# Moving one weight load between two DMA queues at the start of a linear-attention and GEGLU kernel, and reordering the first key matmuls to suit

## Chip, cores, metric

The kernel runs on one core of one Trainium2 chip. The metric is device time in microseconds (us), median of several executions. Before the change it was 273.76 us (three runs, 273.72 to 274.07). A profile's span is about 1.3 us shorter than the time of the same execution, because it counts from the first to the last instruction.

## The reference, cut to what matters

```python
x = A_x                                    # 1 x 2048 x 640, bf16
g = sigmoid((x * gate_w).sum(-1, keepdims=True))
# A: linear attention, 32 heads of 20; phi(t) = where(t > 0, t + 1, exp(t)) + 1e-6
q, k, v = split(x @ wqkv)                  # wqkv: 640 x 1920
a = (phi(q) @ (phi(k)^T v) / (phi(q) . sum phi(k))) @ wo
# B: gelu(x @ w_gate) * (x @ w_up) @ w_down, 640 -> 1728 -> 640
return g * a + (1 - g) * b
```

The change concerns only the first 8 us: the keys `x @ wk` of the first tiles of 128 tokens. wk is the 640 x 640 key part of wqkv; it is loaded in five chunks of 128 rows (160 KB each), one for each 128-deep step of the contraction. "x tile i" is 128 tokens.

## The kernel before: the parts that matter

The matmuls need x with its columns on the partitions. Tile 0 is loaded plainly and transposed by TensorE (`T`); all later tiles come by a transposing DMA (`load_xT`). Two engines issue the early loads, each in program order: SyncE ("sp", SPq in the profile) and ScalarE ("act", ACTq). Neither waits for anything there, so the order of these lines is the order of issue.

```python
def load_wk(k, eng="sp", after=()):
    dma_in(wk[:, k, :], A_wqkv[k * 128:(k + 1) * 128, 640:1280], [r_wk[k]], reads=after, eng=eng)   # issued at L341

def load_xT(i, after=()):
    P.op("sp", lambda e: e.dma_start_transpose(xT[:, :, i * 128:(i + 1) * 128],
                                               A_x[0, i * 128:(i + 1) * 128, :]), ...)              # L353
# ... (cut)
load_x(0)
load_wk(0)
load_xT(1)
load_wk(3)
load_wk(4)
load_wk(1, "act")
load_wk(2, "act")
# ... (cut: a dummy activation that loads ScalarE's table, the gate weights)
for i in range(2, NQ):          # NQ = 4: x tiles 2 and 3
    load_xT(i)
for k in range(KC):
    load_wq(k)
for i in range(NQ, NT):
    load_xT(i)
```

`KM(n, ks)` multiplies tile n by the chunks ks of wk: two matmuls for a chunk, 512 columns (L453) and 128 columns (L454), summed in PSUM (the buffer that takes the results of matmuls) over the five chunks. `warm` runs matmuls on constants, to have TensorE busy before data are there. The order on TensorE is:

```python
warm(5, 512)
warm(1, 128)
T(0, [0], 7)
T(0, [1, 2, 3, 4], 6)
warm(2, 128)
for k in range(3):
    KM(0, [k])
for k in range(3):
    KM(1, [k])
KM(0, [3])
KM(1, [3])
gate_col()
KM(0, [4])
KM(1, [4])
# then keys of tiles 2 and 3, queries of tiles 0 to 3, keys and queries of tiles 4 to 15, ...
```

Of the kernel before, what the change touches and what calls it, by code (L numbers as in the profile page):

```python
# [162 lines left out]
def bass_gated_mix__linear_attn_block__geglu_ffn__prompt_kernel(  # L163
# [63 lines left out]
    with (  # L227
# [8 lines left out]
        with contextlib.ExitStack() as stack:  # L236
# [12 lines left out]
            def new_dma_key():  # L249
                k = "in%d" % dma_next[0]  # L250
                dma_next[0] += 1
                return k
# [16 lines left out]
            wk = wkq[:, :, 0:640]  # L269
# [40 lines left out]
            r_wk = [P.sb("wk%d" % k, R_WK + k * WW, R_WK + k * WW + 640) for k in range(KC)]  # L310
# [29 lines left out]
            def dma_in(dst, src, writes, reads=(), eng="sp"):  # L340
                P.op(eng, lambda e, dst=dst, src=src: e.dma_start(dst, src),  # L341
                     reads=reads, writes=writes, dma=new_dma_key())
# [3 lines left out]
            def load_x(i, eng="sp"):  # L346
                dma_in(x_aug[:, i, 0:640], A_x[0, i * 128:(i + 1) * 128, :], [r_xn[i]], eng=eng)

            def load_wk(k, eng="sp", after=()):
                dma_in(wk[:, k, :], A_wqkv[k * 128:(k + 1) * 128, 640:1280], [r_wk[k]], reads=after, eng=eng)  # L350

            def load_xT(i, after=()):
                P.op("sp", lambda e: e.dma_start_transpose(xT[:, :, i * 128:(i + 1) * 128],  # L353
                                                           A_x[0, i * 128:(i + 1) * 128, :]),
                     reads=list(after), writes=[r_xT[i]], dma=new_dma_key())

            def load_wq(k, eng="sp"):
# [4 lines left out]
                 writes=[P.res("touch")], dma=new_dma_key())  # L362
            load_x(0)
            load_wk(0)
            load_xT(1)
            load_wk(3)
            load_wk(4)
            load_wk(1, "act")
            load_wk(2, "act")

            zero = nc.const_aps.tensor(0.0, (128, 1), F32)
            P.op("act", lambda e: e.activation(eg[:, 0:1], zero, ACT.Exp), writes=[r_eg[0]])
# [15 lines left out]
            for c in range(NHC):  # L388
# [9 lines left out]
                 reads=[r_ones], writes=[r_ident])  # L398
# [16 lines left out]
            def warm(count, n):  # L415
                def fn(e):
                    last = None
                    for w in range(count):
                        last = e.matmul(ps[:, 4, 0:n], one_l, one_r[:, 0:n], start=True, stop=True)
                    return last  # L420
                P.op("pe", fn, writes=[bank[4]])
# [4 lines left out]
            def slot(n):  # L426
                return SLOTS[n % 4]
# [17 lines left out]
            def KM(n, ks):  # L445
                i = seq[n][1]
                b0, b1 = slot(n)

                def fn(e):
                    last = None  # L450
                    for k in ks:
                        lhs = xT[:, k, i * 128:(i + 1) * 128]
                        e.matmul(ps[:, b0, :], lhs, wk[:, k, 0:512], start=(k == 0), stop=(k == KC - 1))  # L453
                        last = e.matmul(ps[:, b1, 0:128], lhs, wk[:, k, 512:640],  # L454
                                        start=(k == 0), stop=(k == KC - 1))
                    return last
                P.op("pe", fn, reads=[r_xTa[i] if i < NXN and ks == [0] else r_xT[i]] + [r_wk[k] for k in ks],
                     writes=[bank[b0], bank[b1]])
# [37 lines left out]
            def gate_col():  # L496

                P.op("pe", lambda e: e.matmul(ps[:, 7, 0:5], gw_sb, ident[:, 0:5], start=True, stop=True),
                     reads=[r_gw, r_ident], writes=[bank[7]])
                P.op("dve", lambda e: e.tensor_copy(wq[:, :, 640:641], ps[:, 7, 0:5].unsqueeze(2)),  # L500
                     reads=[bank[7]], writes=[r_gcol])
# [4 lines left out]
            T(0, [0], 7)  # L506
            T(0, [1, 2, 3, 4], 6)
            warm(2, 128)
            for k in range(3):
                KM(0, [k])  # L510
            for k in range(3):
                KM(1, [k])
            KM(0, [3])
            KM(1, [3])
            gate_col()
            KM(0, [4])
            KM(1, [4])
# [48 lines left out]
            for i in range(NQ, NT):  # L566
                KQ(i)
                if i == 4:
                    late_constants()
            P.op("dve", lambda e: e.tensor_scalar(gg, eg, 0.5, 0.5, ALU.mult, ALU.add),  # L570
                 reads=r_eg, writes=[r_g])
            P.op("dve", lambda e: e.tensor_scalar(omg, eg, -0.5, 0.5, ALU.mult, ALU.add),
                 reads=r_eg, writes=[r_omg])
# [7 lines left out]
                 reads=[r_omg], writes=[r_od], dma=new_dma_key())  # L581
# [44 lines left out]
            def ME(g):  # L626
# [6 lines left out]
                for c in cs:  # L633
# [8 lines left out]
                 reads=r_pk[0:2], writes=[r_tmp[0]])  # L642
            for i in range(2, NT):
                P.op("dve", lambda e, i=i: e.tensor_tensor(zacc, zacc, pk[i], ALU.add),  # L644
                     reads=[r_tmp[0], r_pk[i]], writes=[r_tmp[0]])
# [283 lines left out]
```

## Time and profile before

| what | value | view |
|---|---|---|
| time | 273.76 us | times |
| span, TensorE (PE) busy | 272.6 us, 98% | page |
| keys of tiles 0 and 1 done | 7.70 us | timeline |
| x tile 2 issued, landed | 4.14, 8.07 us | chain of waits |
| keys of tile 2 begin | 8.12 us | timeline |

A load is "issued" when its engine begins to hand it to the DMA queue, and has "landed" when the profile shows it complete.

From the page of the kernel before: the span, the busy time of each engine, and the engines' shares of the chain that ended last.

```profile
span 272.6 us, 3416 instructions
...
PE 267.6 (98%) x1341; PEld 127.9 (47%) x1367; DVE 140.8 (52%) x247; ACT 75.9 (28%) x132; POOL 30.0 (11%) x28
...
PE 96%; DMA 1%; SPq 1%; issue 1%; DVE 0%
```

TensorE is the bound, and almost all of the span is its own work. What loads can cost is only what they cost at the start.

The chain of waits of the same kernel, from 0 to 8.2 us. Columns: start in us, length in us, what the chain passed through. L341 is a plain copy, L353 a transposing load.

```profile
0.79 0.41 SPq L341
...
1.26 0.41 SPq L341
...
1.71 1.30 SPq L353
...
3.06 0.57 SPq L341
...
3.67 0.43 SPq L341
...
4.14 3.93 DMA pool<-in_A_x_dram
...
8.12 0.39 PE ps L453
```

These are x tile 0, wk 0, x tile 1, wk 3, wk 4 and x tile 2, each issued when SyncE is done with the one before. The chain is thus made of issue time (0.41 to 0.57 us for a copy, 1.30 us for a transposing load), and at its end of the 3.93 us from the issue of x tile 2 to its landing.

TensorE in the same profile (timeline; start, length, engine, line, operation, and in brackets the idle time before it with its cause). Lengths overlap, so read the starts.

```profile
4.45 0.58 PE L453 MATMUL ps<-pool 128*128 128x512 bf16 x1 [0.48 <-DMA pool<-in_A_wqkv_dram]
...
4.93 0.51 PE L453 MATMUL ps<-pool 128*128 128x512 bf16 x1
...
5.34 0.38 PE L453 MATMUL ps<-pool 128*128 128x512 bf16 x1
...
5.61 0.38 PE L453 MATMUL ps<-pool 128*128 128x512 bf16 x1
...
7.49 0.22 PE L454 MATMUL ps<-pool 128*128 128x128 bf16 x1
8.12 0.39 PE L453 MATMUL ps<-pool 128*128 128x512 bf16 x1 [0.42 <-DMA pool<-in_A_x_dram]
```

A chunk takes 0.27 us (5.34 to 5.61), but the first ones take 0.48 and 0.41: TensorE is still at a slower early rate. The last key matmul of tiles 0 and 1 ends at 7.49 + 0.22 = 7.71. Then TensorE waits 0.42 us for x tile 2.

The loads of x tiles 1 and 2 in the view of DMA issues (KB are not given for a transposing load; the last number is us from issue to landing):

```profile
pool<-in_A_x_dram SPq DMA_TRANSPOSE x1, 3.8
...
pool<-in_A_x_dram SPq DMA_TRANSPOSE x1, 3.9
```

### The profile page before, as it was taken

What the parts mean: (1) busy time and instruction counts of PE and PEld (TensorE: products, weight loads), DVE (VectorE), ACT (ScalarE), POOL (GpSimd) and SP (SyncE); (2) the same over time, 40 slices, a digit from 0 to 9 for tenths busy, and PEclk for the clock granted to TensorE, in tenths of its full rate; (3) what the DMA queues carried; (4) which work ended last, traced back from release to release, by engine and by line L of the source; (5) the groups of instructions that cost most, each with busy time, mean ns of one, the idle gap of its engine ahead of it and who ended that gap; (6) DMA issues with size and microseconds to landing.
All of it is one profiled execution on the core that took longest, in us unless ns stands there. A gap on an engine that the chain in (4) does not pass through costs nothing.

```text
span 272.6 us, 3416 instructions
## 1 busy us (share of the span) xinstructions
PE 267.6 (98%) x1341; PEld 127.9 (47%) x1367; DVE 140.8 (52%) x247; ACT 75.9 (28%) x132; POOL 30.0 (11%) x28
## 2 busy tenths in 40 slices
PE   8999999999999999999999999999999999999997
PEld 3555555544445454444444444444444444444444
DVE  1678989997233335999999999634210000000200
ACT  2455555210422453232222233224011122121021
POOL 5000000003240002242332422000000000000000
DMA  7976999600200011514121221273031110110211
GB/s 192 202 115 127 346 399 388 140 2 19 58 19 2 23 50 51 192 34 49 26 48 25 49 48 27 60 219 105 5 77 38 41 38 19 38 41 19 58 58 41
DMA packets 42864, 23.78 MB, mean 87 GB/s; under 512 B 32223, under 2 KB 41439, under 8 KB 42719
## 3 DMA queue, kind: packets, MB, share of 16 engines
q1 hardware_dynamic: 42517, 23.22, 31.9%
q10 hardware_dynamic: 330, 0.33, 0.3%
q8 instruction: 11, 0.18, 0.3%
q14 instruction: 6, 0.05, 0.1%
HBM read 13.83 MB, written 2.63 MB: 60 GB/s over the span
## 4 chain that ended last, share of the span: by engine, by line
PE 96%; DMA 1%; SPq 1%; issue 1%; DVE 0%
PE ps L700 41%; PE ps L864 23%; PE ps L539 12%; PE ps L596 6%; PE ps L843 4%; PE ps L468 2%; PE ps L811 2%; PE ps L678 2%; PE ps L599 1%; DMA pool<-in_A_x_dram 1%; PE ps L453 1%; PE ps L824 1%; SPq L341 1%; PE ps L721 1%; SPq L353 0%
## 5 line engine op out<-in xcount | busy, mean ns | idle before, releaser
L700 PE MATMUL ps<-pool 128*128 128x512 bf16 x510 | 113.0, 379 | 0.5
L700 PEld LDWEIGHTS ps<-pool 128*128 128x128 bf16 x520 | 50.5, 98 | 60.0
L864 PE MATMUL ps<-pool 128*128 128x512 bf16 (+2 forms) x300 | 62.4, 366 | 0.3
L706 ACT ACTIVATE pool<-ps 128x512 f32<-128x512 f32 x52 | 31.0, 597 | 73.1 <-PE ps L700 73.1
L708 DVE TENSOR_TENSOR pool<-ps,pool 128x512 bf16<-128x512 f32 x52 | 34.7, 689 | 31.7 <-PE ps L700 30.4
L864 PEld LDWEIGHTS ps<-pool 128*128 128x128 bf16 x306 | 29.2, 98 | 33.4 <-issue 0.4
L847 DVE TENSOR_TENSOR pool<-ps,pool 128x512 bf16<-128x512 f32 x4 | 2.8, 690 | 61.5 <-PE ps L843 61.5
L539 PE MATMUL ps<-pool 128*128 128x512 bf16 (+1 forms) x176 | 32.5, 343 | 0.2
L754 POOL TENSOR_TENSOR pool<-pool 128x640 f32<-128x640 bf16 x16 | 22.4, 1404 | 73.0 <-DVE pool L756 65.6
L871 ACT ACTIVATE pool<-ps,pool 128x512 bf16<-128x512 f32 (+1 forms) x16 | 10.9, 680 | 68.6 <-PE ps L864 68.6
L539 PEld LDWEIGHTS ps<-pool 128*128 128x128 bf16 x180 | 17.6, 98 | 15.0
L558 DVE SCALAR_TENSOR_TENSOR pool<-ps,pool 128x128 bf16<-128x128 f32 (+2 forms) x36 | 21.7, 602 | 2.1
L549 ACT ACTIVATE pool<-ps 128x640 bf16<-128x640 f32 x24 | 16.9, 703 | 15.8 <-DVE pool L558 9.3
L596 PE MATMUL ps<-pool 128*128 128x512 bf16 x76 | 19.2, 379 | 0.1
L764 DVE TENSOR_TENSOR pool<-pool 128x640 bf16<-128x640 bf16 x16 | 13.2, 826 | 0.6
L762 DVE TENSOR_SCALAR pool<-pool 128x32 f32<-128x32 f32 x16 | 12.8, 802 | 0.6
L756 DVE TENSOR_REDUCE pool<-pool 128x32 f32<-128x640 f32 x16 | 12.9, 808 | 0.0
L644 DVE TENSOR_TENSOR pool<-pool 128x640 f32<-128x640 f32 x14 | 11.6, 826 | 0.5
L843 PE MATMUL ps<-pool 128*128 128x512 bf16 x51 | 11.5, 379 | 0.1
L646 POOL PARTITION_ALL_REDUCE pool<-pool x1 | 4.0, 3971 | 61.0 <-DVE pool L644 61.0
L596 PEld LDWEIGHTS ps<-pool 128*128 128x128 bf16 x78 | 7.0, 98 | 7.3
L555 DVE TENSOR_SCALAR pool<-pool 128x640 bf16<-128x640 bf16 x24 | 7.9, 327 | 1.7 <-ACT pool L549 0.4
(70 smaller groups left out, 124.1 us busy)
## 6 DMA issues: line engine op xcount, KB each, us to landing
out_dram<-pool SPq DMA_DIRECT2D x19, 128.0 KB, 1.7
pool<-in_B_w_gate_dram SPq DMA_DIRECT2D x1, 2080.0 KB, 14.8
pool<-in_B_w_up_dram SPq DMA_DIRECT2D x1, 2080.0 KB, 18.0
pool<-in_A_wqkv_dram SPq DMA_DIRECT2D x8, 160.0 KB, 3.1
pool<-in_A_x_dram SPq DMA_DIRECT2D x1, 1280.0 KB, 9.2
pool<-in_A_x_dram SPq DMA_DIRECT2D x1, 1120.0 KB, 6.3
pool<-in_B_w_down_dram SPq DMA_DIRECT2D x1, 1120.0 KB, 6.4
pool<-omg_row SPq DMA_DIRECT2D x1, 1024.0 KB, 4.8
```

Of the source, the lines that this page charges most:

```text
L539: last = e.matmul(ps[:, b + p, 0:c1 - c0], xT[:, k, i * 128:(i + 1) * 128], wkq[:, k, c0:c1], start=(k == 0), stop=(k == KC - 1))
L549: P.op("act", lambda e: e.activation(e_buf[m], ps_flat[:, o:o + 640], ACT.Exp), reads=banks, writes=[r_e[m]])
L558: P.op("dve", lambda e, c0=c0, c1=c1: e.scalar_tensor_tensor(dst[:, c0:c1], ps_flat[:, o + c0:o + c1], 1.0 + EPS, e_buf[m][:, c0:c1], ALU. ...
L596: last = e.matmul(ps[:, b, :], pk[i][:, c * 128:(c + 1) * 128], x_aug[:, i, 0:512], start=(i == 0), stop=(i == NT - 1))
L700: last = e.matmul(ps[:, b, :], w[:, k, fc * 128:(fc + 1) * 128], xT[:, k, j * 512:(j + 1) * 512], start=(k == 0), stop=(k == KC - 1))
L706: P.op("act", lambda e: e.activation(ge[n], ps[:, gb, :], ACT.Gelu_apprx_tanh), reads=[bank[gb]], writes=[r_ge[n]])
L708: P.op("dve", lambda e: e.tensor_tensor(hT[fc][:, j * 512:(j + 1) * 512], ps[:, ub, :], ge[n], ALU.mult), reads=[bank[ub], r_ge[n]], write ...
L754: P.op("pool", lambda e: e.tensor_tensor(tmp[n], pq[i], z_b, ALU.mult), reads=[r_pq[i], r_zb], writes=[r_tmp[n]])
L756: P.op("dve", lambda e: e.tensor_reduce(den[n], tmp[n].rearrange("p (h d) -> p h d", h=32), AX.X, ALU.add), reads=[r_tmp[n]], writes=[r_de ...
L764: P.op("dve", lambda e: e.tensor_tensor(pq[i].rearrange("p (h d) -> p h d", h=32), pq[i].rearrange("p (h d) -> p h d", h=32), den[n].unsqu ...
L843: last = e.matmul(ps[:, b, :], wd[:, fc, 512:640], hT[fc][:, j * 512:(j + 1) * 512], start=False, stop=(fc == NFC - 2), skip_group_check=True)
L864: last = e.matmul(ps[:, pb, 0:c1 - c0], lhs, rhs, start=False, stop=(q == len(rows) - 1), skip_group_check=True)
```

## The change

It takes wk 2 out of ScalarE's queue and puts it behind x tile 1 in SyncE's. So wk 2 should no longer compete with x tile 1's data for the DMA engines; x tile 1 then may land earlier, and keys of tile 1 may start earlier. The key matmuls are reordered because wk 2 now comes after x tile 1: tile 0 by chunks 0 and 1, tile 1 by chunks 0 and 1, then chunk by chunk.

```diff
-            def load_wk(k, eng="sp", after=()):
+            def load_wk(k, eng="sp"):
             load_x(0)
             load_wk(0)
             load_xT(1)
+            load_wk(2)
             load_wk(3)
             load_wk(4)
             load_wk(1, "act")
-            load_wk(2, "act")
 # ... (cut)
             warm(2, 128)
-            for k in range(3):
+            for k in range(2):
                 KM(0, [k])
-            for k in range(3):
+            for k in range(2):
                 KM(1, [k])
-            KM(0, [3])
-            KM(1, [3])
+            for k in (2, 3):
+                KM(0, [k])
+                KM(1, [k])
             gate_col()
             KM(0, [4])
             KM(1, [4])
```

More of the change, by code (lines that the diff above doesn't have):

```diff
@@ L347, in load_x @@
                 dma_in(x_aug[:, i, 0:640], A_x[0, i * 128:(i + 1) * 128, :], [r_xn[i]], eng=eng)
-            def load_wk(k, eng="sp", after=()):
-                dma_in(wk[:, k, :], A_wqkv[k * 128:(k + 1) * 128, 640:1280], [r_wk[k]], reads=after, eng=eng)
+            def load_wk(k, eng="sp"):
+                dma_in(wk[:, k, :], A_wqkv[k * 128:(k + 1) * 128, 640:1280], [r_wk[k]], eng=eng)
             def load_xT(i, after=()):
```

## The prediction

> **What bounds the kernel.** TensorE. The page gives PE busy 267.6 of a 272.6 us span (98%); the chain of waits puts 96% on PE. Only the first 8.12 us can change. In the timeline PE idles there about 0.5 us before 4.45 (waiting for wk 0) and 0.42 us before 8.12. After 16.50 it never waits for a load.
>
> The chain shows what sets 8.12: not wk, but SyncE's queue. It issues x tile 0 at 0.79, wk 0 at 1.26, the transposing load of x tile 1 at 1.71 (1.30 us), wk 3 at 3.06, wk 4 at 3.67, x tile 2's transposing load at 4.14, which lands 3.93 us later (8.07). The key matmuls of tiles 0 and 1 had ended at 7.70: wk has slack, x tile 2's issue has none.
>
> **What the change does.**
> 1. One more copy, wk 2, stands in SyncE's queue before x tile 2. Such issues took 0.41 to 0.57 us. So wk 3, wk 4, x tiles 2 and 3 and all later loads are issued 0.45 us later (x tile 2 at about 4.6).
> 2. ScalarE's queue loses one copy of 0.45 us, but it idles 3.78 us before its first exponential: worth nothing.
> 3. wk 2 no longer competes with x tile 1's data. The DMA engines are about saturated from 3.1 to 6.4 us (share near 1 in the windows); 160 KB fewer ahead is worth, at the 267 to 356 GB/s there, 0.45 to 0.6 us. x tile 1 (landed at 5.5) may land near 5.1.
> 4. The key matmuls only change order; a chunk costs 0.27 us warm, as before. wk 2 takes wk 3's old place (landed at 6.4), so PE probably waits some tenths for it after tile 1's chunks 0 and 1. Tiles 0 and 1 end at 7.5 to 7.9 instead of 7.70.
>
> **On the critical path.** Only x tile 2's landing. If its 3.93 us is pure latency after issue, it lands 0.45 us later (8.5). If part of it is queueing (the fastest transposing load of this trace landed in 2.9 us), the later issue is absorbed, as the bytes in front are the same in total. The Trainium skill, page "DMA: Bandwidth & Descriptors", section "Issuing engines are not separate DMA queues", says that all issuers share the same 16 DMA engines and that issuing from several saves only sequencer time; here that time is what the chain is made of. I expect 0.3 us lost, and no later slack to give it back: x tile 3 and the wq chunks have 0.4 us or more to spare, and PE is full to the end.
>
> **Prediction.** 274.05 us against 273.76; 8 times in 10 between 273.6 and 274.6. Faster by over 2%: 0.005; within 2%: 0.99; slower by over 2%: 0.005.
>
> **What would show it.** SyncE's queue: x tile 2 issued at 4.6. Timeline: tile 2's key matmuls begin at 8.1 to 8.6 after a PE idle of 0.3 to 0.9 us put down to the x load; small waits for wk before it; everything after shifted alike.
>
> **What would make it wrong.** wk 4 landing after 7.5 us, which puts wk on the chain; a gap that keeps TensorE longer at its slow early rate (512-column matmuls are spaced 0.43 us before 5.2 us, 0.22 after); wq arriving late for the first query tile; or x tile 2 landing earlier because ScalarE's second copy no longer shares the engines.

## The result and the profile after

The median was 274.07 us (six runs, 273.96 to 274.62) against 273.81 us for the kernel before in the same session (six runs). The ratio is 1.0012, with a 95% interval of 0.9999 to 1.0024: the same within 2%. Ratios are the mean time of one kernel's fast runs over the mean of the other's fast runs of the same rounds, so they are not quite the ratio of the medians.

The page of the kernel after:

```profile
span 272.8 us, 3442 instructions
```

SyncE's queue after (timeline; start, length, instruction, how many in a row):

```profile
0.79 0.40 SPq L341 DMA_DIRECT2D pool<-in_A_x_dram  x1
1.25 0.41 SPq L341 DMA_DIRECT2D pool<-in_A_wqkv_dram  x1
1.71 1.31 SPq L353 DMA_TRANSPOSE pool<-in_A_x_dram  x1
3.07 1.52 SPq L341 DMA_DIRECT2D pool<-in_A_wqkv_dram  x3
4.63 2.52 SPq L353 DMA_TRANSPOSE pool<-in_A_x_dram  x2
```

As predicted, three wk copies stand there instead of two, and x tile 2 is issued at 4.63 instead of 4.14. The loads of x tiles 1 and 2:

```profile
pool<-in_A_x_dram SPq DMA_TRANSPOSE x1, 3.4
...
pool<-in_A_x_dram SPq DMA_TRANSPOSE x1, 3.5
```

x tile 1 lands at 1.71 + 3.4 = 5.1 instead of 5.5, and x tile 2 at 4.63 + 3.5 = 8.13 (the view rounds the 3.5) instead of 8.07: most of its later issue was given back by a shorter way to landing. So far this reads as "fully absorbed". But tile 2's keys begin 0.19 us later, and not because of x tile 2 (TensorE, timeline):

```profile
5.37 0.63 PE L453 MATMUL ps<-pool 128*128 128x512 bf16 x1
...
5.90 0.63 PE L453 MATMUL ps<-pool 128*128 128x512 bf16 x1
...
6.43 0.60 PE L453 MATMUL ps<-pool 128*128 128x512 bf16 x1
...
6.92 0.38 PE L453 MATMUL ps<-pool 128*128 128x512 bf16 x1
...
8.25 0.22 PE L454 MATMUL ps<-pool 128*128 128x128 bf16 x1
8.31 0.38 PE L453 MATMUL ps<-pool 128*128 128x512 bf16 x1
```

No wait stands in brackets. Chunks take 0.53 us up to 6.4 us, twice the later 0.27: in this execution the slow rate lasted until about 6.9 us, against about 5.2 in the profile of before. TensorE had work all the time up to 8.31, so this profile does not show what the change did to the waits. The same 0.2 us are in the span (272.8 against 272.6). In both profiles the span is the start of tile 2's keys plus 264.5 us: after that point nothing changed.

Three explanations were left. **Half absorbed** (the prediction, which put 0.3 of 0.45 us as lost): the later issue of x tile 2 costs part of its 0.49 us. **Warm-up by chance**: the end of the slow rate differs from run to run, and x tile 2 costs nothing. **Warm-up by cause**: the new order makes the slow rate last longer.

### The profile page after: what moved, and what is told of

Its sections match the earlier page's. It is cut to its first block, busy times and chain, and to the rows that moved or that the text cites. A ratio compares the mean times of both kernels' runs of the same rounds, so it can differ in the third digit from the quotient of the medians.

```text
span 272.8 us, 3442 instructions
## 1 busy us (share of the span) xinstructions
PE 269.8 (99%) x1367; PEld 128.2 (47%) x1367; DVE 140.6 (52%) x247; ACT 76.0 (28%) x132; POOL 30.0 (11%) x28
## 4 chain that ended last, share of the span: by engine, by line
PE 99%; DVE 0%; issue 0%
PE ps L701 41%; PE ps L865 23%; PE ps L540 12%; PE ps L597 6%; PE ps L844 4%; PE ps L453 2%; PE ps L468 2%; PE ps L812 2%; PE ps L679 2%; PE ps L600 1%; PE ps L419 1%; PE ps L825 1%; PE ps L722 1%; PE ps L454 0%; PE ps L740 0%; PE ps L469 0%
```

## Experiments

### Both kernels again

Edit: none. Each ran a second time, later the changed one a third time, each with a new profile.

> The kernel before, unchanged, a second time: how much do time and profile of one kernel vary? Theory Q (queue): the time is set by x tile 2's landing at 8.07 us, so tile 2's keys begin at about 8.12 again and the ratio to before is 1.0000 within 0.0005. Theory W (warm-up): the moment at which TensorE leaves its slow early rate (5.2 us in the first profile of before, 6.9 us in that of after) differs from run to run of one kernel; then this profile may show another moment, anywhere from about 4.5 to 7.5 us, and if it is later than about 6.0 us the keys of tile 2 begin after 8.12 us, up to 8.9.

> The changed kernel, unchanged, a second time. Theory W (the 0.26 us are the late end of the slow rate, by chance): if this profile leaves the slow rate near 5.2 us, tile 2's keys begin at the landing of x tile 2, about 8.15 to 8.2 us, and the execution is as fast as before; the median of the rounds comes out within 0.1 us of before's. Theory Q (the later issue of x tile 2 costs): the median is again 0.2 to 0.4 us above before's. Theory C (the changed loads or order themselves make the slow rate last longer): the slow rate ends near 6.9 us again, and again the median is 0.2 to 0.4 us above.

> The changed kernel a third time, for more timed runs beside before on the same chip and one more profile. So far before has a median of 273.9 us and after of 274.0 to 274.1. Theory half absorbed (x tile 2, issued 0.48 us later, lands 0.1 to 0.3 us later): the median is 0.1 to 0.3 us above before's of the same call; x tile 2 lands 3.4 to 3.7 us after its issue, x tile 1 3.3 to 3.5 us after its own. Theory warm-up alone: no difference of the medians over 0.05 us in the long run, and any difference is explained by the moment at which the slow rate ends.

| session | before, median (runs) | after, median (runs) | difference of medians | ratio, 95% interval |
|---|---|---|---|---|
| result | 273.81 (6) | 274.07 (6) | 0.26 | 1.0012, 0.9999 to 1.0024 |
| second | 273.92 (9) | 274.01 (5) | 0.09 | 1.0003, 0.9989 to 1.0017 |
| third | 274.00 (11) | 274.15 (5) | 0.15 | 1.0005, 0.9988 to 1.0022 |

The repeat of before itself gave 273.83 us and a ratio of 0.9999. Every interval contains 1, so no single session proves a difference. All three have the same sign, and of before's 31 runs (the repeat counted) 12 are under 273.88 us, which is the lowest of after's 16. Pooled, the medians are 273.92 and 274.075 us. So a small difference, some 0.15 us, is likely; these times do not tell its cause.

The profiles show the rest. In the repeat of before the slow rate was over by 4.78 us, and something else set the pace (chain of waits):

```profile
1.71 4.38 DMA pool<-in_A_x_dram
6.09 0.05 issue
6.14 0.39 PE ps L453
```

Here x tile 1 took 4.38 us, behind wk 1 and wk 2 of the other queue. Keys of tile 1 could not begin before 6.14, and from there TensorE was the chain up to tile 2's keys at 8.23. This is the wait that the change was made for. It cost little here: the trace has x tile 2 landing at 8.18 us in this execution, so without it tile 2's keys could have begun at most 0.05 us earlier. In the four profiles of the changed kernel or its loads without a hold-back (first, second, third, and the loads alone below) x tile 1 took 3.3 to 3.5 us.

The third profile of after has an early end of the slow rate (chunks of 0.27 us already at 4.46), and it is the one that the prediction described (chain of waits, then one line of the timeline):

```profile
3.07 0.57 SPq L341
...
3.68 0.44 SPq L341
...
4.16 0.43 SPq L341
...
4.63 3.64 DMA pool<-in_A_x_dram
...
8.32 0.39 PE ps L453
```

```profile
8.32 0.39 PE L453 MATMUL ps<-pool 128*128 128x512 bf16 x1 [0.41 <-DMA pool<-in_A_x_dram]
```

There are three copies in front of x tile 2, it lands at 8.28, and TensorE waits 0.41 us for it. The second profile of after had tile 2's keys at 8.13, right after x tile 2 (landed at 8.09); TensorE had been idle for 0.06 us. So "warm-up by cause" falls in its plain form: with the same kernel the slow rate ended at about 6.9, 5.4 and before 4.46. Whether the new order makes a late end more frequent cannot be told from three profiles. Chance moves the start of tile 2's keys by some tenths in either kernel.

### Both kernels with TensorE warmed up first

Edit, the same in both kernels: VectorE runs a chain of 11 additions on a scratch tile (`z_b`), the first load of each queue waits for it, and TensorE runs a long warm-up in the meantime. This holds all loads back to 12.19 us and leaves their order as it is.

```diff
+            P.op("dve", lambda e: e.memset(z_b, 0.0), writes=[r_zb])
+            for _n in range(11):
+                P.op("dve", lambda e: e.tensor_tensor(z_b, z_b, z_b, ALU.add), reads=[r_zb], writes=[r_zb])
 # the first DMA of each queue also gets reads=[r_zb]
-            warm(5, 512)
+            warm(24, 512)      # 36 in the second pair
+            P.op("pe", <one 128-column matmul>, reads=[r_zb], writes=[bank[4]])
+            warm(9, 512)
             warm(1, 128)
```

> The kernel before with all loads held back by about 9 us (a chain of 11 additions on VectorE of 0.83 us each) while TensorE runs 24 warm-up matmuls of 512 columns, so that TensorE is at its fast rate when the keys begin. The time is about 9 us more than before; it is to be compared with the next run only. Expected in every theory: from x tile 0's issue on, x tile 2 is issued 3.35 us and lands 7.28 us later, and tile 2's keys begin 7.33 us later (as in the first profile of before: 8.12 - 0.79), with a TensorE idle of 0.4 us or more (about 1 us) before them.

> The changed kernel with the same hold-back and the same long warm-up, to be compared with the run before. Theory Q pure (the landing follows the issue): tile 2's keys begin 7.8 us after x tile 0's issue, 0.45 us later than in the run before, and the time is 0.45 us longer. Absorbed (the bytes in front are the same; in the profile of after x tile 2 landed at 8.13 against 8.07): 7.4 us after, and the time is longer by at most 0.1 us; the 0.26 us of the unheld kernels are then the slow rate's, theories W or C.

> The held-back kernel before once more, with 36 instead of 24 warm-up matmuls, because the run with 24 left TensorE idle for 3.1 to 4.4 us before the loads and one of the two profiles fell back to the slow rate. Loads are released at 12.19 us again. Expected: all key matmuls at the fast rate (0.22 us between 512-column matmuls of one chain); x tile 2 is issued at 15.56, lands 3.9 to 4.0 us later, tile 2's keys begin at 19.5 (19.28 in the first such run).

> The changed kernel held back with 36 warm-up matmuls; to be compared with the run before it. Pure latency of the issue: x tile 2, issued at 16.02, lands 3.9 us later and tile 2's keys begin at 19.9 to 20.0, the median 0.4 us or more above the run before. Absorbed: it lands 3.5 us after its issue, tile 2's keys begin within 0.1 us of the run before, and so does the median (noise about 0.15 us).

The first pair missed its aim. With 24 warm-up matmuls TensorE stood idle before the release, for 3.08 us in the one kernel and 4.42 us in the other, and the second had fallen back to the slow rate (its ten following warm-up matmuls took 4.15 us against 2.19). Its medians, 285.42 and 285.52 us, tell nothing. With 36 matmuls the idle time was 1.64 and 1.66 us and both were fast. Tile 2's keys, first in the held-back kernel before, then in the changed one (timeline; the lines of the kernel moved to L456 and L457):

```profile
19.10 0.22 PE L457 MATMUL ps<-pool 128*128 128x128 bf16 x1
19.19 0.39 PE L456 MATMUL ps<-pool 128*128 128x512 bf16 x1
```

```profile
19.35 0.22 PE L457 MATMUL ps<-pool 128*128 128x128 bf16 x1
19.66 0.39 PE L456 MATMUL ps<-pool 128*128 128x512 bf16 x1
```

In this pair the changed kernel is 0.47 us later, the whole of the issue delay: x tile 2 took 3.6 us in both. That was not expected: the kernel before should have needed 3.9 to 4.0 us here as in its first profile, and why it did not is open. The medians of five runs (285.97 and 285.67 us) even have the other sign, with ranges of 0.7 and 1.1 us. In the profile of the held-back kernel before, the last wq chunk landed late and gave its lead back (TensorE waited 0.25 us for it at 24.5 us). The hold-back takes the slow rate out of one profile, but not the noise out of the times.

All profiles of the two kernels together, x tile 2 counted from the issue of x tile 0:

| profile | x tile 2 issued | issue to landing | landed |
|---|---|---|---|
| before, first | 3.35 | 3.93 | 7.28 |
| before, again | 3.36 | 4.0 | 7.4 |
| before, held back, 24 | 3.37 | 3.67 | 7.04 |
| before, held back, 36 | 3.37 | 3.6 | 7.0 |
| after, first | 3.84 | 3.5 | 7.3 |
| after, again | 3.83 | 3.47 | 7.30 |
| after, third | 3.84 | 3.64 | 7.48 |
| after, held back, 24 | 3.83 | 4.0 | 7.8 |
| after, held back, 36 | 3.85 | 3.57 | 7.42 |

The means are about 7.2 for before and 7.5 for after (7.4 without the profile whose TensorE had cooled down), so of 0.48 us of later issue some 0.2 to 0.3 us arrive at the landing. But this mean mixes two unlike groups. In the kernels as they are (two profiles of before, three of after) the landing came under 0.1 us later in the mean, and tile 2's keys began 0.08 us later. In the held-back pair with 36 matmuls nothing was absorbed: the landing came 0.4 us later. One kernel's own profiles differ by 0.4 us or more. How much of the later issue is absorbed in an ordinary execution is therefore not fixed by these profiles.

### The issue alone

Edit to the kernel before: one tiny copy in SyncE's queue in front of x tile 2, everything else as it was.

```diff
             load_wk(4)
+            P.op("sp", lambda e: e.dma_start(touch[0:16, 8:12], A_wqkv[0:128:8, 640:644]),
+                 writes=[P.res("touch2")], dma=new_dma_key())
             load_wk(1, "act")
```

> The kernel before with one tiny copy (16 rows of 8 bytes) put into SyncE's queue just before x tile 2: wk 2 stays in ScalarE's queue, the bytes in front of x tile 2 stay the same, only its issue comes about 0.45 us later (4.6). Pure latency: x tile 2 lands at 8.5 and the median is 0.3 to 0.45 us above before. Queueing on the DMA engines: it lands 3.5 us after its issue at about 8.1 to 8.2, and the median is within 0.15 us of before.

The median was 274.20 us against 273.92 for before: 0.28 us, ratio 1.0019 (0.9994 to 1.0044). (Two of the eleven runs of before beside it stood far out, 275.15 and 579.51 us; the median hardly feels them.) x tile 2 was issued at 4.63. The profile fell on an execution of 276.02 us, while the other five took 274.12 to 274.34: wk 0 landed 3.69 us after its issue instead of 3.1, and the slow rate lasted to about 10.0 us. So its 3.7 us for x tile 2 is no good evidence. The times suggest that the later issue alone costs about 0.3 us, no less than the change as a whole: eight of before's runs beside it lie under 274.12, the lowest of its six. The times lie nearer to the "pure latency" value (0.3 to 0.45) than to "queueing" (under 0.15); the interval leaves both possible.

### The cleared queue alone

Edit: wk 2 leaves ScalarE's queue but goes behind x tile 2, and its chunk is computed last for tiles 0 to 2. x tile 2 keeps the issue time of before.

```diff
             load_xT(1)
-            load_wk(2)
             load_wk(3)
             load_wk(4)
 # ...
-            for i in range(2, NQ):
-                load_xT(i)
+            load_xT(2)
+            load_wk(2)
+            load_xT(3)
 # ... (matmuls: last chunk of tiles 0 to 2 is chunk 2)
-            for k in (2, 3):
-                KM(0, [k])
-                KM(1, [k])
+            KM(0, [3])
+            KM(1, [3])
             gate_col()
             KM(0, [4])
             KM(1, [4])
+            KM(2, [0, 1, 3, 4])
+            for n in range(3):
+                KM(n, [2])
```

> The other half of the change alone: wk 2 leaves ScalarE's queue, but x tile 2 keeps its issue time of 4.14, because wk 2 is issued behind x tile 2 (at about 5.4) and chunk 2 of tiles 0, 1 and 2 is computed last. 160 KB fewer are in front of x tile 2 than in both kernels. Theory half absorbed (landing depends on both the issue and the traffic in front): x tile 1 lands 3.3 to 3.5 us after its issue as in after, x tile 2 3.3 to 3.6 us after its own, at about 7.5 to 7.7 instead of 8.07, and wk 2 by 8.5. TensorE then has the same work left as before when it starts tile 2's keys (four chunks of it first, two of tiles 0 and 1 after), so the time is within 0.15 us of before's. If the landing followed the issue alone it would stay at 8.07 and tile 2's keys would begin there with two chunks of tiles 0 and 1 still to do: 0.4 to 0.5 us slower than before.

The landings came as expected. x tiles 1 and 2 in this kernel (DMA issues):

```profile
pool<-in_A_x_dram SPq DMA_TRANSPOSE x1, 3.4
...
pool<-in_A_x_dram SPq DMA_TRANSPOSE x1, 3.3
```

x tile 2, issued at 4.14, landed at about 7.45. With the same issue time, 3.3 us stand against 3.6 to 4.0 in the four profiles of before: 160 KB fewer in front were worth 0.3 to 0.7 us. So the bytes in front do count. But this is not what the change does for x tile 2: in the changed kernel wk 2 still stands in front of it, with the same total of bytes as before. Only x tile 1 (3.4 us in both) is cleared in the same way.

The time did not come as expected: 275.03 us, ratio 1.0044 (1.0030 to 1.0058), where I had expected it within 0.15 us of before. The keys of tiles 0 to 3 ended at 10.97 against 11.01 us in before, so up to there the expectation held. But tiles 0 and 1 were finished at 9.1 and 9.3 us instead of 7.4 and 7.7, and their way through the exponential and the two VectorE operations now stood in front of the query matmuls that need their PSUM banks (chain of waits):

```profile
9.11 0.71 ACT pool L479
...
10.21 0.82 DVE pool L493
...
11.30 0.84 DVE pool L493
...
12.18 0.39 PE ps L469
```

An order of matmuls that is free for TensorE was not free for the engines behind it.

### More loads in ScalarE's queue

Edit to the kernel before: wk 3 and wk 4 go to ScalarE's queue, so that x tile 2 is issued at 3.06.

```diff
-            load_wk(3)
-            load_wk(4)
             load_wk(1, "act")
             load_wk(2, "act")
+            load_wk(3, "act")
+            load_wk(4, "act")
```

> The opposite direction: the kernel before with wk 3 and wk 4 moved from SyncE's queue to ScalarE's, behind wk 1 and wk 2. x tile 2 is issued at 3.06 instead of 4.14 and no longer stands behind them in its own queue. If issue and queue position set its landing, it lands at about 7.0 to 7.3, tile 2's keys follow the others without a gap (about 7.7 at an early fast rate), and the median is up to 0.4 us below before. If only the total of bytes counts, wk 4 or x tile 2 still lands near 8 us and the median stays within 0.15 us.

It was slower than before, though within 2%: 276.09 us, ratio 1.0078 (1.0041 to 1.0114). The loads of x tiles 1 and 2:

```profile
pool<-in_A_x_dram SPq DMA_TRANSPOSE x1, 5.5
...
pool<-in_A_x_dram SPq DMA_TRANSPOSE x1, 5.2
```

x tile 1 now takes 5.5 us, and x tile 2, issued 1.1 us earlier than in before, lands at 3.06 + 5.2, about 8.2 us, no earlier than in before (8.07 and 8.18). TensorE's keys of tile 1 could begin only at 7.22. With no wk, with wk 2, and with wk 2 to 4 behind wk 1 in ScalarE's queue, x tile 1 took 3.3 to 3.5, 3.8 to 4.5, and 5.5 us (without a hold-back). The Trainium skill, page "DMA: Bandwidth & Descriptors", section "Queues, rings and completion order", says that "each SDMA engine round-robins between the queue rows it has work for, at *packet* granularity". These numbers fit it: the more loads stood in the other queue, the longer x tile 1 took. They do not show the packets' turns themselves.

### wk 0 in ScalarE's queue

Edit to the changed kernel, to give SyncE's queue its issue time back while wk 2 stays out of the way: `load_wk(0)` is taken from its place and `load_wk(0, "act")` put in front of `load_wk(1, "act")`.

> The changed kernel with wk 0 moved from SyncE's queue to the head of ScalarE's, in front of wk 1. SyncE's queue gets shorter by one copy: x tile 1 is issued at 1.26 and x tile 2 at 4.15 again, as in the kernel before, while wk 2 stays out of x tile 1's way. If issue time and clean engines both count: x tile 1 lands by 5.0, x tile 2 at about 7.7, and the median is 0.1 to 0.4 us below before's, better than both kernels. If the total of bytes alone counts, x tile 2 lands at 8.1 again and the median is within 0.1 us of before's. It could lose if wk 0 and wk 1, now sharing the engines with x tile 1, land later than 4.6 us.

x tile 1 was issued at 1.26 and x tile 2 at 4.17, as intended, but it lost against before: 274.75 us, ratio 1.0034 (1.0013 to 1.0055). TensorE (timeline):

```profile
6.33 0.38 PE L453 MATMUL ps<-pool 128*128 128x512 bf16 x1 [1.35 <-DMA pool<-in_A_wqkv_dram]
```

wk 1 landed only 4.5 us after its issue at 1.7, and TensorE waited 1.35 us for it. Now wk 0 and wk 1 stood in the other queue beside x tile 1, which took 4.7 us itself. x tile 2, with the issue time and the bytes of before in front of it, landed at 8.13, as in before (8.07 and 8.18), and not at the hoped-for 7.7. This version was meant to beat both kernels and does not. The miss that the expectation had named, wk landing late beside x tile 1, is what came.

### The loads without the new order

Edit: the changed loads with the old order of the key matmuls.

> The changed loads with the old order of key matmuls (tile 0's chunks 0 to 2, then tile 1's). TensorE must wait for wk 2, which lands at about 6.0 us, as its third piece of key work, and has 8 pieces of 0.27 us left: they end at 8.2 us or later at the fast rate (7.7 in the kernel before), so keys rather than x tile 2 (8.1 to 8.3) set the start of tile 2's keys, and it is at least as slow as after. With a late end of the slow rate: up to 9 us. Expected median 0.1 to 0.5 us above after's. If it equals after within 0.05 us, the new order was not needed.

The median was 274.69 us, ratio to before 1.0046 (1.0010 to 1.0083), 0.54 us above the changed kernel's 274.15 in the same session (two of six runs took over 276 us). The profile shows the expected reason (timeline):

```profile
6.23 0.39 PE L453 MATMUL ps<-pool 128*128 128x512 bf16 x1 [0.84 <-DMA pool<-in_A_wqkv_dram]
```

TensorE waits 0.84 us for wk 2 as its third piece, works without a gap from there, and tile 2's keys begin at 8.44. In the third profile of after the wait for the same chunk was 0.17 us. But in that profile tile 2's keys began at 8.32, only 0.12 us earlier, and the profiled run of the loads alone is the fastest of the six (274.30 us). So the profile bears the expected reason out for 0.12 us; the rest of the 0.54 us is not explained. The loads do better with the new order.

## Why the prediction was right, point by point

- **Bound and critical path: right.** In every profile of the two kernels as they are, the span is the start of tile 2's keys plus 264.5 us (8.12, 8.23; 8.31, 8.13, 8.32). Nothing later gave the delay back. That only x tile 2's landing matters held in three of these five; in the second of before the wait for x tile 1 came in front, and in the first of after the slow rate.
- **Issue of x tile 2 later by 0.45 us: right**, it was 0.49 (4.14 to 4.63).
- **x tile 1 earlier, near 5.1: right**, 5.0 to 5.2 in the three profiles of after. I called it off the chain; in the second profile of before x tile 1 landed at 6.09 and was on the chain, but there x tile 2 was only 0.05 us behind.
- **Part of the later issue absorbed, 0.3 us lost: right in sign, the size is open.** The medians differ by 0.26, 0.09 and 0.15 us, somewhat less than the 0.29 us predicted (274.05 against 273.76), and each interval still contains no difference. That the first session met the prediction to 0.02 us is luck. The issue alone cost 0.28 us in the median, so the later issue may account for the whole loss. That x tile 2 landed 3.3 instead of 3.6 to 4.0 us after its issue when wk 2 was out of its way shows that part of its time is queueing, which is the prediction's reason for absorption. How much was absorbed differs: by the landings, most of it in the kernels as they are, nothing in the held-back pair.
- **Small waits for wk before tile 2: right but minor**, 0.17 us for wk 2 in the third profile. Tiles 0 and 1 ended at 8.5, 8.1 and 7.9 us, where 7.5 to 7.9 was predicted; the slow rate, which held up the first two, was not in that sum. wk 4 held nothing up in the changed kernel; in the third profile it landed at 7.15, just before its first use at 7.21.
- **What the first profile of after showed was not the predicted picture.** No wait for x stood before tile 2's keys; the slow early rate did. The prediction listed a longer slow rate as a danger and gave a gap as its cause. The profiles bear the cause out only in part: before the keys TensorE idled 0.35 us in the first profile of after, which was slow for long, and 0.72 us in the repeat of before, which was not. But the two longest such gaps, 0.89 us (more loads in ScalarE's queue) and 1.06 us (the issue alone), came with the two latest ends, 8.9 and 10.0 us. The end lay anywhere between before 4.46 and 10.0 us. What decides it in a given run is open. A single profile of each kernel would have led to a wrong story.

## What to carry to other kernels

An early load's landing depended here on two things that trade against each other: when its queue issues it, and how many bytes of any queue are in front of it; shifting a small load between queues changes both and may move nothing. Test the two apart (a tiny dummy copy for the issue, the load put behind for the bytes) before believing either. For tenths of a microsecond at the start of a kernel take several profiles of the same kernel, because TensorE's warm-up alone moves the chain by as much (0.1 to 0.2 us in the first profile of after).

## What the Trainium skill lacked or had wrong

- "TensorE: Matmul & The Clock Gate", Part 1, puts the end of the slow rate "around 4µs into sustained matmul activity, ±500ns run-to-run", and says that the window is free-running. Counted from the first matmul at 0.82 us, the profiles here have it at under 3.7 us (third of after), about 4.4 (first of before), 6.0 (first of after) and about 9.1 us (the issue alone, with a wait of 1.06 us in between): a wider range. The activity was not sustained, though: in all four TensorE idled before the keys, 0.35 us or more. The profile's granted-clock figure is 1.0 for all these executions, so it does not show the slow rate at the start; the spacing of the matmuls does.
- The same page, "Why this matters for your kernels", warns of idle gaps over about 3 us. It agrees: after 3.08 us of idle TensorE was still fast, after 4.42 us slow. This second slow stage does show in the granted clock, 0.50 from 13.0 to 16.3 us.
- "DMA: Bandwidth & Descriptors", "Rules for kernel authors", says that spreading loads over SP and ACT does not help bandwidth, because they interleave on the same engines, and only saves issue time. It does not say that it can hurt: x tile 1's transposing load went from 3.4 to 5.5 us when the other queue held four wk chunks instead of one.
- The same page has no issue time of a transposing load of this shape on this chip (128 x 640 bf16 from HBM); its count for one from HBM is for small tiles only. SyncE took 1.2 to 1.3 us for one at the start of these kernels, against 0.41 to 0.57 us for a plain copy of the same size. One transposing load thus held the queue as long as two or three copies.
